# Own buffers for one batch's local queries and keys, a packed third Fourier tile, and a later place for one output scaling

## The chip, the cores and the metric

The kernel runs on one core of a Trainium2 chip. The metric is the device time of one execution in microseconds (us), as the median of several runs; less is better. One execution was also recorded by the hardware profiler, and the rows further down are from that one.

A core has engines that each work through an instruction stream of their own in order: TensorE (PE in the profile; PEld is its weight load, which overlaps), VectorE (DVE), ScalarE (ACT), GpSimd (POOL), and SyncE (SP), which here only issues transfers. Streams wait for each other by semaphores. Transfers are carried by 16 DMA engines.

## What is computed

```python
# q, k, v: 4 batches x 8 heads x 576 x 64
rel = pos[:, None] - pos[None, :]
mask_local = (rel >= 0) & (rel < 32)                       # heads 0 to 3
mask_strided = (rel >= 0) & (pos[None, :] % 32 == pos[:, None] % 32)   # heads 4 to 7
x = softmax(where(mask, q @ k.T / 8, -1e9)) @ v            # 576 x 512 for each batch
u = x + real(fft(fft(x, axis=1), axis=2))                  # over sequence and channels
un = (u - mean(u)) / sqrt(var(u) + 1e-6)
x2 = u + relu(un @ w_ch1) @ w_ch2                          # 512 -> 2048 -> 512
h = relu(x2.T @ w_tok1) @ w_tok2                           # over the sequence, 576 -> 256 -> 576
u2 = x2 + h.T
out = u2 + relu(u2 @ w_ch3) @ w_ch4                        # 512 -> 1536 -> 512
```

All is float32. The big weights come as pairs of 32-bit words, from which the kernel builds its numbers on ACT, DVE and POOL.

## The kernel before

**Attention, the first 147 us.** Each batch has six groups (`Group`, 24 in the list `gl`): three of local heads, each with two tiles of 96 queries against a window of 128 keys, and three of strided heads, where the positions are ordered so that those with equal remainder by 32 stand together (tiles of 126 or 108 positions). A group computes scores on PE (`scores`: a matmul that puts the mask into PSUM, then one per head and tile, `sc<-k,qz`), the maximum on DVE and the exponentials on ACT (`softmax`), transposes the result on PE (`trans`, tile `tp`), multiplies it by the values (`av`), and scales by the sum of the exponentials (`out`, on DVE, lines L262 to L264). `out` also stores the rows to the scratch `xd`. Two heads share 128 partitions of `k`. So that one matmul takes one head alone, the query tile `qz` has zeros in the other head's 64 rows; the zeros are set once at the start (L518), and the loads write the live rows only.

**The loads of queries and keys.** `load_qk(b, g, pool)` issues for batch b two loads of `qz[g]` and one of the keys `k`; g is 0 for local and 1 for strided heads. Both kinds have one buffer, so a load waits until the scores of the batch before have read it. In the loop over the groups the local set of the next batch is loaded in front of a batch's fourth group, and its strided set in front of its own first group. All these loads are on SP, in program order with the stores of `xd`, the loads and stores of the Fourier stage and the weight loads `wraw` (L101). The program gives SP's transfers eight completion counters in turn, so an issue also waits for the transfer that stands eight places before it. The constants `cs`, `ss`, `cd`, `sd` (cosines and sines as high and low parts) are issued by POOL's queue behind the values of the first batch.

**The Fourier stage (`Fourier`).** While batch b+1 is in attention, batch b is transformed; the fourth batch's transform stands in the MLP stage behind. `load` reads `xa` (rows from the front of the sequence) and `xr` (the mirror rows) in three tiles of 128, 128 and 33 rows; `prep` adds them to `e` on DVE and splits the sum in a high part (ACT, L317) and a low part (POOL, L318) in the tile `f`; `s1` multiplies by the cosines or sines in five column blocks (`g<-cs,f`, L334): in each of the first four there are nine matmuls, three tiles by high x high, high x low, low x high, and the fifth block, one column, has six. `s2` multiplies over the channels and stores the three tiles of `u` to the scratch `ud`. When these steps come is set by a small table in `fft(b)`, which ties each of them to a group's matmul or reduction.

**The first norm and the MLP.** In group 17's turn the first three tiles of `u` are loaded (`us`, L447), in group 19's turn `ln_stats` computes their mean and inverse root on DVE (L471 and, in `inverse_root`, a chain of small instructions that ends at L478); groups 20 to 22 apply it, and behind the last group the tiles are transposed to `uT`, which opens the MLP: `h<-uT,wAh` (L413), `hh` on ACT (L417), `hl` on DVE (L418), `oo` (L432). Here PE multiplies high and low parts, three products each. The second block (token mixing and its own MLP) follows.

The order in which the instructions of one engine stand is worked out by a scheduler when the kernel is built, from the program's order, the dependences and the ties given by `behind`.

## Time and profile before

| | us |
|---|---|
| three runs | 926.74, 932.41, 928.37 |
| median | 928.37 |
| profiled execution, its own time | 922.47 |
| its span, first to last instruction | 920.7 |
| PE busy | 892.5 (97%) |
| DVE busy | 560.0 (61%) |
| ACT busy | 408.3 (44%) |
| POOL busy | 313.0 (34%) |

161 MB were moved. The mean granted clock of PE was 0.994 of full speed, which is the upper of its two levels (2.4 GHz). Busy shares are means over stages with different limits; PE's 97% leaves 28 us of the span without PE work, start and end included.

### The profile page before, as it was taken

Reading aid. Unit: us, or ns where it says so; the run is one execution under the profiler, and the core shown is the slowest. Engines: PE = TensorE matmul, PEld = TensorE weight load, DVE = VectorE, ACT = ScalarE, POOL = GpSimd, SP = SyncE. Lnnn points to the kernel's source line nnn. Section 1 sums busy time; section 2 is a strip of 40 time slices with the busy share of each in tenths; the row PEclk is TensorE's granted clock in tenths of the full one; section 3 lists DMA queues with packets and bytes.
Section 4 is the critical chain, followed back from the end, with each engine's and each line's share of the span. In section 5 each row is a group of like instructions: output and inputs, shape, how many; then the busy total and the mean of one; then the engine's idle time right before and its main releaser. Section 6 shows DMA issues by size and latency. Waiting matters only on the chain.

```text
span 920.7 us, 15422 instructions
## 1 busy us (share of the span) xinstructions
PE 892.5 (97%) x5554; PEld 824.2 (90%) x5554; DVE 560.0 (61%) x1046; ACT 408.3 (44%) x1069; POOL 313.0 (34%) x372
## 2 busy tenths in 40 slices
PE   7989989999999999999999999999999999999997
PEld 6979988999998989998888897777899999999997
DVE  4667979798894434443443446645434444888774
ACT  5978776353442333233223224323455545444432
POOL 3122222332330133344444333422223001946660
PEclk9989999999999999999999999999999999999999
DMA  9997864234431354644744665579833287156351
GB/s 260 282 289 216 255 205 136 98 127 146 138 111 68 99 160 146 196 128 126 220 141 136 209 200 180 176 262 313 293 120 147 104 270 243 36 161 222 125 203 47
DMA packets 116972, 161.00 MB, mean 175 GB/s; under 512 B 9662, under 2 KB 70180, under 8 KB 116896
## 3 DMA queue, kind: packets, MB, share of 16 engines
q1 hardware_dynamic: 114928, 157.29, 54.0%
q0 software_dynamic: 1712, 2.51, 1.1%
q8 instruction: 44, 0.72, 0.3%
q14 instruction: 32, 0.26, 0.1%
q10 hardware_dynamic: 256, 0.21, 0.1%
HBM read 104.92 MB, written 55.06 MB: 174 GB/s over the span
## 4 chain that ended last, share of the span: by engine, by line
PE 63%; DVE 11%; DMA 9%; ACT 5%; issue 4%; POOL 4%; SPq 3%; POOLq 0%; DVEq 0%; ACTq 0%
PE oo L1036 14%; PE oo L432 10%; PE h L413 10%; PE z L895 8%; PE y L895 4%; DMA wraw<-in_w1b_dram 4%; POOL wt L147 3%; PE tu L806 3%; PE tk L784 3%; PE sc L211 2%; PE w L895 2%; SPq L101 2%; DVE wu L112 2%; DVE wu L108 2%; DVE wu L113 2%
## 5 line engine op out<-in xcount | busy, mean ns | idle before, releaser
L413 PE MATMUL h<-uT,wAh 128*128 128x384 f32 x768 | 203.1, 337 | 0.2
L413 PEld LDWEIGHTS h<-uT,wAh 128*128 128x128 f32 x768 | 139.0, 188 | 5.2 <-PE g L334 0.4
L1036 PE MATMUL oo<-wo,ht 128*128 128x256 f32 x972 | 133.7, 281 | 0.0
L413 PE MATMUL h<-uT,wAl 128*128 128x384 f32 x384 | 129.0, 336 | 0.0
L1036 PEld LDWEIGHTS oo<-wo,ht 128*128 128x128 f32 x972 | 126.5, 189 | 0.0
L432 PE MATMUL oo<-wAh,hh 128*128 128x512 f32 x288 | 113.9, 398 | 4.3 <-ACT hh L417 4.2
L432 PE MATMUL oo<-wAl,hh 128*128 128x512 f32 x288 | 113.7, 395 | 0.0
L432 PE MATMUL oo<-wAh,hl 128*128 128x512 f32 x288 | 104.4, 396 | 0.2 <-DVE hl L418 0.2
L418 DVE SCALAR_TENSOR_TENSOR hl<-h,hh 128x384 fp32r<-128x384 f32 x96 | 52.6, 552 | 76.0 <-ACT hh L417 75.8
L108 DVE TENSOR_SCALAR wu<-wu 128x512 f32<-128x512 f32 (+1 forms) x62 | 38.5, 622 | 78.2 <-ACT wu L106 73.2
L124 POOL TENSOR_TENSOR wAl<-wu,wAh 128x512 fp32r<-128x512 f32 x32 | 45.9, 1437 | 104.3 <-ACT wAh L123 104.3
L417 ACT ACTIVATE hh<-h 128x384 fp32r<-128x384 f32 x96 | 45.9, 484 | 70.4 <-PE h L413 68.9
L147 POOL TENSOR_TENSOR wt<-wu 128x128 f32<-128x128 f32 x48 | 21.1, 461 | 158.3 <-DVE wu L113 158.3
L413 PEld LDWEIGHTS h<-uT,wAl 128*128 128x128 f32 x384 | 72.1, 188 | 2.8
L432 PEld LDWEIGHTS oo<-wAh,hh 128*128 128x128 f32 x288 | 54.1, 188 | 15.6 <-ACT hh L417 6.6
L106 ACT ACTIVATE wu<-wraw 128x512 f32<-128x512 f32 (+1 forms) x62 | 41.0, 662 | 60.6 <-DMA wraw<-in_w1b_dram 46.9
L895 PE MATMUL z<-ut,wo 128*128 128x384 f32 x324 | 64.5, 338 | 1.7 <-DVE ut L863 1.7
L432 PEld LDWEIGHTS oo<-wAh,hl 128*128 128x128 f32 x288 | 53.8, 188 | 13.7 <-DVE hl L418 1.3
L432 PEld LDWEIGHTS oo<-wAl,hh 128*128 128x128 f32 x288 | 54.1, 188 | 8.9
L230 ACT ACTIVATE sm<-sc,st 96x128 f32<-96x128 f32 (+2 forms) x176 | 61.6, 373 | 0.6
L895 PEld LDWEIGHTS z<-ut,wo 128*128 128x128 f32 x324 | 56.4, 188 | 2.1 <-DVE ut L863 2.0
L211 PE MATMUL sc<-k,qz 128*96 128x128 f32 (+2 forms) x352 | 51.0, 283 | 5.3 <-DMA k<-in_kt_dram 5.3
(197 smaller groups left out, 1840.9 us busy)
## 6 DMA issues: line engine op xcount, KB each, us to landing
wo<-wsd SPq DMA_DIRECT2D x84, 256.0 KB
wsd<-wraw SPq DMA_DIRECT2D x24, 448.0 KB
wsd<-wbl SPq DMA_DIRECT2D x24, 448.0 KB
u<-u2d SPq DMA_DIRECT2D x36, 256.0 KB
hd<-hs SPq DMA_DIRECT2D x12, 768.0 KB
hw<-hd SPq DMA_DIRECT2D x36, 256.0 KB
wraw<-in_w1a_dram SPq DMA_DIRECT2D x16, 512.0 KB
wraw<-in_w2a_dram SPq DMA_DIRECT2D x16, 512.0 KB
```

Source lines behind the costliest of these rows:

```text
L106: behind(nc.scalar.activation(out=f32(u), in_=f32(high), func=AF.Abs, scale=2.0**16), relu.get("hh"))
L108: clamp = eng().tensor_scalar(f32(u), f32(u), E_MIN, E_MAX, op0=ALU.max, op1=ALU.min)
L124: nc.gpsimd.tensor_tensor(out=lo[:, :n], in0=u, in1=f32(hi[:, :n]), op=ALU.subtract)
L147: nc.gpsimd.tensor_tensor(out=o, in0=x, in1=y, op=ALU.add if plus else ALU.subtract)
L211: last = nc.tensor.matmul(out=sc[:q, j * k:(j + 1) * k], lhsT=qz[self.g][:, e, hp, qs], rhs=k_t[self.b, self.g][:, hp, ks], start=False, s ...
L230: self.exp = nc.scalar.activation(out=smv[:, j, :], in_=sc[:, j, :], func=AF.Exp, scale=SCALE, bias=st[:, 1, j:j + 1], accum_out=st[:, 2, ...
L413: nc.tensor.matmul(out=h[:, :384], lhsT=l[:, ws], rhs=r[:, kd, :], start=x == 0, stop=x == 11)
L417: relu["hh"] = nc.scalar.activation(out=hh, in_=h[:, :384], func=AF.Relu)
L418: relu["hl"] = nc.vector.scalar_tensor_tensor(out=hl, in0=h[:, :384], scalar=0.0, in1=f32(hh), op0=ALU.max, op1=ALU.subtract)
L432: nc.tensor.matmul(out=self.o[c][i], lhsT=l[:, s], rhs=r, start=first and x == 0, stop=last and x == 2)
L895: Unit.last = nc.tensor.matmul(out=bank[:, :384], lhsT=w[:, c + kd * P:c + kd * P + P], rhs=r[:, kd], start=first and x == 0, stop=x == 5, ...
L1036: nc.tensor.matmul(out=acc[G][bank][:, 256 * half:256 * half + 256], lhsT=lh[:, i], rhs=w[:, c:c + 256], start=m == 0 and x == 0 and half ...
```

## The change

1. *Buffers.* The local keys `k` have two buffers instead of one, and the second batch's local queries go to four tiles of their own, `qo`, which lie in buffers that `u` uses later. Their zeros are set at the start like those of `qz`. The second batch's local set is loaded at the start of the program (`load_qk(1, 0, ap)`); in the loop, the first batch's fourth group now loads the third batch's local set, and the third batch's fourth group the fourth's. The second batch's fourth group loads none.
2. *Third Fourier tile.* The rows are regrouped: tiles 0 and 1 hold rows 1 to 256 (and their mirror rows), tile 2 the 33 rows left. The high and low parts of tile 2 share one operand `f3` of 128 partitions (rows 0 to 32 the high part, 64 to 96 the low part, and from 96 on, over the low part's last row, the high part again), with a fifth constant tile that holds the matching rows; one matmul then does what three did (in the one-column block two). ACT writes one more copy for each batch. Because the 33 rows are no longer one piece in memory, `load` and the stores of tile 2 have six transfers each; tiles 0 and 1 have one for each half. `cs` and `ss` are one transfer each instead of four.
3. *Scaling.* The 21st group's scaling (`out` of `gl[20]`) is put behind the last instruction of the first norm's chain.

```diff
-        t = pool.tile([P, 2, S], F32, tag=f"k{g}", name="k", bufs=(1, 1)[g])
+        t = pool.tile([P, 2, S], F32, tag=f"k{g}", name="k", bufs=(2, 1)[g])
         k_t[b, g] = t
+        own = b == 1 and g == 0
         for ps in ([slice(0, 1), slice(1, 2)] if b == 0 and g < 1 else [slice(0, 2)]):
             for e in range(2):
                 r = slice(64 * e, 64 * e + 64)
-                nc.sync.dma_start(out=qz[g][r, e, ps], in_=a["qt"][b, g, r, ps])
+                if own:
+                    for hp in range(2):
+                        nc.sync.dma_start(out=qo[e, hp][r], in_=a["qt"][b, g, r, hp])
+                else:
+                    nc.sync.dma_start(out=qz[g][r, e, ps], in_=a["qt"][b, g, r, ps])
...
-                nc.vector.tensor_scalar_add(rs, rs, 1e-9)
+                behind(nc.vector.tensor_scalar_add(rs, rs, 1e-9), self.prev)
...
+        def rows(self, i):
+            xa, xr = self.x[i]
+            if i < 2:
+                return (xa, 0, 1 + 128 * i, 128), (xr, 0, 288 + 128 * i, 128)
+            return ((xa, 32, 0, 1), (xa, 1, 257, 15), (xa, 16, 272, 16),
+                    (xr, 0, 575, 1), (xr, 1, 544, 15), (xr, 16, 559, 16))
...
-            behind(nc.scalar.activation(out=f[:n, 0, i], in_=e[:n], func=AF.Copy), prev2)
-            nc.gpsimd.tensor_tensor(out=f[:n, 1, i], in0=e[:n], in1=f32(f[:n, 0, i]), op=ALU.subtract)
+            h, l = (f[:, 0, i], f[:, 1, i]) if i < 2 else (f3[0:33], f3[64:97])
+            behind(nc.scalar.activation(out=h, in_=e[:n], func=AF.Copy), prev2)
+            if i == 2:
+                behind(nc.scalar.activation(out=f3[96:128], in_=e[0:32], func=AF.Copy), prev2)
+            nc.gpsimd.tensor_tensor(out=l, in0=e[:n], in1=f32(h), op=ALU.subtract)
...
-            for i in range(3):
+            for i in range(2):
+                h, l = f[:, 0, i, c], f[:, 1, i, c]
                 if mt < 4:
-                    h, l = f[:, 0, i, c], f[:, 1, i, c]
-                    mats += [(h, w[0][:, i], m), (h, w[1][:, i], m), (l, w[0][:, i], m)]
+                    mats += [(h, w[:, i], m), (h, w[:, 2 + i], m), (l, w[:, i], m)]
                 else:
-                    mats += [(f[:, :, i, 256], w[0][:, i], 2), (f[:, 0, i, 256:257], w[1][:, i], 1)]
+                    mats += [(f[:, :, i, 256], w[:, i], 2), (h, w[:, 2 + i], 1)]
+            mats.append((f3[:, c], w[:, 4], 128 if mt < 4 else 1))
...
-            na = min(n, 288 - r0)
-            nc.sync.dma_start(out=ud[self.b][287 + r0:287 + r0 + n, :], in_=xr[:n])
-            nc.sync.dma_start(out=ud[self.b][r0:r0 + na, :], in_=xa[:na])
+            for t, p0, r0, k in self.rows(i)[::-1]:
+                nc.sync.dma_start(out=ud[self.b][r0:r0 + k, :], in_=t[p0:p0 + k])
...
+        for e in range(2):
+            for hp in range(2):
+                qo[e, hp] = lp.tile([P, S], F32, tag="u", name="qo", bufs=6)
+                nc.vector.memset(qo[e, hp][64 - 64 * e:128 - 64 * e], 0.0)
         load_vl(0)
         load_qk(0, 1, ap)
         vlast = load_vs(0)
-
-        cs = [fp.tile([P, 3, 290], F32R, name=f"cs{i}") for i in range(2)]
-        ss = [fp.tile([P, 3, 290], F32R, name=f"ss{i}") for i in range(2)]
+        load_qk(1, 0, ap)
+
+        cs, ss = (fp.tile([P, 5, 290], F32R, name=nm) for nm in ("cs", "ss"))
...
+        for t, nm in ((cs, "cs"), (ss, "ss")):
+            nc.gpsimd.dma_start(out=t, in_=a[nm])
         for i in range(2):
-            for t, w in ((cs[i], a["cs"][i]), (ss[i], a["ss"][i])):
-                nc.gpsimd.dma_start(out=t[:, 0:2], in_=w[:, 0:2])
-                nc.gpsimd.dma_start(out=t[:33, 2], in_=w[:33, 2])
...
             if gi == 3 and b + 1 < B:
-                load_qk(b + 1, 0, ap)
+                if b != 1:
+                    load_qk(2 if b == 0 else 3, 0, ap)
                 load_vl(b + 1)
...
             if gno == 19:
                 mvs = ln_stats(us, lp, g.red[1])
+                gl[20].prev = relu["ln"]
```

The rows of the order below are an engine's instructions as they stand one behind the other: the line in the kernel, the operation, output and inputs with the shape, and a count where like rows follow each other. The line numbers of the changed kernel are its own.

The first place is SP's stream in the opening, behind the first batch's loads and up to the keys of the second batch's strided set. Here `qz_140` is the local query tile and `qz_139` the strided one, and `xd` are the first batch's stores. Before:

```order
L101 DMA wraw<-in_w1a_dram 128x1024
L101 DMA wraw<-in_w2a_dram 128x1024
L101 DMA wraw<-in_w1a_dram 128x1024
L176 DMA qz_140<-in_qt_dram 64x1152
L271 DMA xd_69<-x 96x2x256
L176 DMA qz_140<-in_qt_dram 64x1152
L177 DMA k<-in_kt_dram 128x1152
L271 DMA xd_69<-x 96x2x256
L180 DMA vl<-in_vl_dram 128x1536
L271 DMA xd_69<-x 96x2x256
L176 DMA qz_139<-in_qt_dram 64x1152 x2
L177 DMA k<-in_kt_dram 128x1152
```

And now:

```order
L179 DMA qo<-in_qt_dram 64x576 x4
L182 DMA k<-in_kt_dram 128x1152
L101 DMA wraw<-in_w1a_dram 128x1024
L101 DMA wraw<-in_w2a_dram 128x1024
L101 DMA wraw<-in_w1a_dram 128x1024
L181 DMA qz_140<-in_qt_dram 64x1152
L277 DMA xd_69<-x 96x2x256
L181 DMA qz_140<-in_qt_dram 64x1152
L182 DMA k<-in_kt_dram 128x1152
L277 DMA xd_69<-x 96x2x256
L185 DMA vl<-in_vl_dram 128x1536
L277 DMA xd_69<-x 96x2x256
```

The four `qo` loads and a set of keys, which are the second batch's, stand ahead of all; the pair of `qz_140` and the keys that follow it stand where they stood, and now carry the third batch's rows. The strided set follows these rows, as before.

The second place is SP at the end of the first batch's Fourier transform: its last stores of `u` (`ud`) and the loads of the first norm (`u`). Before:

```order
L376 DMA ud_73<-xa 32x512
L101 DMA wraw<-in_w1a_dram 128x1024
L375 DMA ud_73<-xr 33x512
L447 DMA u<-ud_73 128x512
L183 DMA vs<-in_vs_dram 126x1280
L447 DMA u<-ud_73 128x512
L277 DMA xd_71<-x 9x6x256
L278 DMA xd_71<-x 9x6x256
L447 DMA u<-ud_73 64x512
```

And now:

```order
L388 DMA ud_73<-xa 16x512
L388 DMA ud_73<-xa 15x512
L388 DMA ud_73<-xr 16x512
L388 DMA ud_73<-xr 15x512
L388 DMA ud_73<-xr 1x512
L388 DMA ud_73<-xa 1x512
L283 DMA xd_71<-x 9x6x256
L284 DMA xd_71<-x 9x6x256
L459 DMA u<-ud_73 128x512 x3
```

Six stores stand where two stood, and the three loads of `u` stand behind the two `xd` stores, where two of them stood ahead.

The third place is DVE at the end of the attention, from the last instructions of the norm's chain (`nr`, `mv`); `x<-av,st` is a group's scaling, `xa<-xa,m` belongs to the Fourier stage. Before:

```order
L464 SCALAR_TENSOR_TENSOR mv<-nr,mv 128x3
L478 SCALAR_TENSOR_TENSOR mv<-mv 128x3
L264 TENSOR_TENSOR x<-av,st 96x512
L367 TENSOR_TENSOR m<-sa,fb 128x258
L368 TENSOR_TENSOR m<-sa,fb 128x258
L373 TENSOR_TENSOR xa<-xa,m 128x512
L373 TENSOR_TENSOR xr<-xr,m 128x512
L227 TENSOR_REDUCE st<-sc 126x4
L312 TENSOR_TENSOR w<-xa,xr 128x510
L313 TENSOR_TENSOR e<-xa,xr 128x2
L315 TENSOR_TENSOR e<-w 128x255
L264 TENSOR_TENSOR x<-av,st 96x512
```

And now:

```order
L474 SCALAR_TENSOR_TENSOR nr<-mv,nr 128x3
L269 RECIPROCAL st<-st 108x4
L475 TENSOR_TENSOR nr<-nr,mv 128x3
L476 SCALAR_TENSOR_TENSOR mv<-nr,mv 128x3
L490 SCALAR_TENSOR_TENSOR mv<-mv 128x3
L268 TENSOR_SCALAR st<-st 96x8
L269 RECIPROCAL st<-st 96x8
L270 TENSOR_TENSOR x<-av,st 96x512
L270 TENSOR_TENSOR x<-av,st 126x512
L270 TENSOR_TENSOR x<-av,st 108x512
L270 TENSOR_TENSOR x<-av,st 108x256
L415 TENSOR_TENSOR uT<-ut,uT 128x4x128 x3
```

Before, the scalings of the last groups were spread between other work; now four of them stand in a row behind the norm's chain and ahead of the instructions that form `uT`.

## Rows read from the trace of the kernel before

**Rows 1.** The page's 40 slices of the span, busy tenths of PE in each.
```profile
PE   7989989999999999999999999999999999999997
```

**Rows 2.** The waits of PE, of SP in 8:60, of DVE in 40:170: us, times, longest.
```profile
PE sc L211 <- DMA k<-in_kt_dram: 5.3, 2, 4.4
...
PE oo L432 <- ACT hh L417: 4.2, 6, 1.1
...
SPq L278 <- DMA k<-in_kt_dram: 1.0, 1, 1.0
...
DVE bs L471 <- DMA u<-ud: 3.4, 2, 2.6
```

**Rows 3.** The timeline of PE: start us, duration us, instruction, idle time before it.
```profile
7.73 4.65 PE L211 MATMUL sc<-k,qz 128*96 128x128 f32 x24 [0.93 <-DMA k<-in_kt_dram]
...
39.03 1.04 PE L211 MATMUL sc<-k,qz 128*96 128x128 f32 x8
...
43.25 1.04 PE L211 MATMUL sc<-k,qz 128*126 128x126 f32 x8
...
55.02 0.46 PE L205 MATMUL sc<-mask_l,ident_r 96*96 96x512 f32 x1
...
59.83 1.99 PE L211 MATMUL sc<-k,qz 128*96 128x128 f32 x8 [4.36 <-DMA k<-in_kt_dram]
...
147.52 1.39 PE L413 MATMUL h<-uT,wAh 128*128 128x384 f32 x3
```

**Rows 4.** Windows: engines' busy us (instructions), then granted clock, DMA share, GB/s.
```profile
8.00:40.00 32.00, 31.82 (x283) 29.96 (x283) 17.41 (x40) 27.43 (x143) 7.23 (x14) 1.00 1.11 305
...
44.00:48.00 4.00, 4.00 (x43) 3.93 (x42) 2.59 (x6) 4.00 (x19) 1.27 (x1) 1.00 0.46 119
...
60.00:64.00 4.00, 4.00 (x19) 3.85 (x20) 1.50 (x6) 0.82 (x3) 0.00 (x0) 0.50 1.04 411
...
64.00:68.00 4.00, 4.00 (x33) 3.93 (x32) 3.48 (x8) 2.30 (x14) 1.29 (x1) 0.78 1.04 253
...
70.00:110.00 40.00, 38.84 (x349) 37.11 (x348) 35.23 (x74) 31.39 (x139) 10.27 (x8) 1.00 0.79 239
```

**Rows 5.** The timeline of POOL's and SP's transfer issues: start us, duration of the issue.
```profile
31.79 0.54 POOL L541 DMA_DIRECT2D sd<-in_sd_dram  x1
...
42.81 0.75 SPq L278 DMA_DIRECT2D xd<-x  x1
...
52.98 0.57 SPq L177 DMA_DIRECT2D k<-in_kt_dram  x1
...
110.98 0.33 SPq L375 DMA_DIRECT2D ud<-xr  x1
```

**Rows 6.** Transfers issued in 0:60: count, KB each, us from issue to landing.
```profile
qz<-in_qt_dram SPq DMA_DIRECT2D x10, 288.0 KB
...
k<-in_kt_dram SPq DMA_DIRECT2D x5, 576.0 KB
...
cs<-in_cs_dram POOLq DMA_DIRECT2D x2, 290.0 KB, 11.1
...
cs<-in_cs_dram POOLq DMA_DIRECT2D x2, 37.4 KB, 11.1
...
sd<-in_sd_dram POOLq DMA_DIRECT2D x2, 258.0 KB, 12.2
```

**Rows 7.** Lines by form in 0:221: busy us, mean ns, idle before.
```profile
L317 ACT ACTIVATE f<-e 33x512 fp32r<-33x512 f32 x4 | 2.5, 628 | 1.1 <-DVE e L316 1.1
...
L518 DVE MEMSET qz<- 64x576 f32 x4 | 2.2, 538 | 0.7 <-issue 0.7
```

**Rows 8.** The chain that ended last: start us, duration us, piece.
```profile
109.96 1.76 DMA ud<-xa
...
144.45 0.52 ACT f L317
...
192.63 2.42 PE g L334 x18
```

More of the change, by code (lines that the diff above doesn't have):

```diff
@@ L211, in scores @@
                         last = nc.tensor.matmul(
-                            out=sc[:q, j * k:(j + 1) * k], lhsT=qz[self.g][:, e, hp, qs],
+                            out=sc[:q, j * k:(j + 1) * k], lhsT=(qo[e, hp] if (self.b, self.g) == (1, 0) else qz[self.g][:, e, hp])[:, qs],
                             rhs=k_t[self.b, self.g][:, hp, ks], start=False, stop=j == n - 1)
@@ L291, in load @@
             self.x[i] = xa, xr
-            na = min(n, 288 - r0)
             if i == 2:
-                nc.gpsimd.memset(xa[32:33], 0.0)
-            if i == 0:
-                nc.gpsimd.memset(xr[0:1], 0.0)
-            nc.sync.dma_start(out=xa[:na], in_=xd[self.b][r0:r0 + na, :])
-            for c0, c1 in ([(1, 16), (16, n)] if i == 0 else [(0, n)]):
-                self.last = nc.sync.dma_start(out=xr[c0:c1], in_=xd[self.b][287 + r0 + c0:287 + r0 + c1, :])
+                nc.gpsimd.memset(xa[0:1], 0.0)
+                nc.gpsimd.memset(xr[32:33], 0.0)
+            for t, p0, r0, n in self.rows(i):
+                self.last = nc.sync.dma_start(out=t[p0:p0 + n], in_=xd[self.b][r0:r0 + n, :])
+        def rows(self, i):
[4 more added lines that the diff above has]
+                    (xr, 0, 575, 1), (xr, 1, 544, 15), (xr, 16, 559, 16))
         def prep(self, i, prev=None, prev2=None):
-            r0, n = ST[i]
-            f = self.f = self.k["f"]
+            n = NR[i]
+            f, f3 = self.k["f"]
             xa, xr = self.x[i]
@@ L441, in u_tile @@
             if c % 3 < 2:
-                return self.lp.tile([P, DM], F32, tag="u", name="u", bufs=6)
+                return self.lp.tile([P, S], F32, tag="u", name="u", bufs=6)[:, :DM]
             return self.pool.tile([P, DM], F32, tag="v", name="v", bufs=3)
@@ L477, in ln_stats @@
             nc.vector.reciprocal(out=mv[:, :n, 3], in_=mv[:, :n, 2])
-        nc.vector.scalar_tensor_tensor(out=mv[:, :n, 2], in0=mv[:, :n, 0], scalar=-1.0, in1=mv[:, :n, 3],
-                                       op0=ALU.mult, op1=ALU.mult)
+        relu["ln"] = nc.vector.scalar_tensor_tensor(out=mv[:, :n, 2], in0=mv[:, :n, 0], scalar=-1.0,
+                                                    in1=mv[:, :n, 3], op0=ALU.mult, op1=ALU.mult)
         return [mv[:, i] for i in range(n)]
@@ L527, in attention_fourier_mlp_kernel @@
         alt = fp.tile([P, 258], F32R, name="alt")
-        f = fp.tile([P, 2, 3, 512], F32R, name="f")
+        f = fp.tile([P, 2, 2, DM], F32R, name="f"), fp.tile([P, DM], F32R, name="f3")
         g4 = [fp.tile([P, 290], F32R, name=f"g4{x}") for x in "hl"]
@@ L531, in attention_fourier_mlp_kernel @@
         tc.add_manual_dep(tick.ins, vlast.ins.name, mybir.DependencyInfo(mybir.DependencyClass.Sync, mybir.DependencyReason.DATA), reason="constants behind the first batch")
-        for t in (g4[1], alt, f[:, 0, 2], f[:, 1, 2], cs[0][:, 2], cs[1][:, 2], ss[0][:, 2], ss[1][:, 2]):
+        for t in (g4[1], alt, f[1][32:64]):
             nc.gpsimd.memset(f32(t), 0.0)
@@ L601, in attention_fourier_mlp_kernel @@
             if gno == 17:
-                us = [u_rows(T, lp.tile([P, DM], F32, tag="u", name="u", bufs=6)) for T in range(3)]
+                us = [u_rows(T, lp.tile([P, S], F32, tag="u", name="u", bufs=6)[:, :DM]) for T in range(3)]
             if gno == 21:
-                us += [u_rows(T, lp.tile([P, DM], F32, tag="u", name="u", bufs=6)) for T in range(3, 6)]
+                us += [u_rows(T, lp.tile([P, S], F32, tag="u", name="u", bufs=6)[:, :DM]) for T in range(3, 6)]
             if gno == 19:
                 mvs = ln_stats(us, lp, g.red[1])
+                gl[20].prev = relu["ln"]
             if 20 <= gno < 23:
@@ L828, in u_load @@
         def u_load(T):
-            u = lp.tile([P, DM], F32, tag="u", name="u", bufs=6)
+            u = lp.tile([P, S], F32, tag="u", name="u", bufs=6)[:, :DM]
             nc.sync.dma_start(out=u, in_=u2d[T // 9][T % 9])
@@ L1054, in halves @@
                 if G == Gs[-1]:
-                    k = lp.tile([P, DM], F32, tag="u", name="k", bufs=6)
+                    k = lp.tile([P, S], F32, tag="u", name="k", bufs=6)[:, :DM]
                     nc.scalar.activation(out=k, in_=t, func=AF.Copy)
@@ L1157, in trig @@
         return v
-    s = np.arange(289)
+    s = np.concatenate([np.arange(1, 257), [288], np.arange(257, 288), [0]])
+    for nm, f in (("cs", np.cos), ("ss", np.sin)):
+        w = np.zeros((289, 290))
+        w[:, :289] = trig(f, 576, s, s)
+        h, l = _split(w)
+        t = np.zeros((P, 5, 290), np.float32)
+        t[:, 0:2], t[:, 2:4] = (x[:256].reshape(2, P, 290).transpose(1, 0, 2) for x in (h, l))
+        t[0:33, 4], t[64:97, 4], t[97:128, 4] = h[256:], h[256:], l[257:288]
+        c[nm] = t
     full = {}
-    for nm, f in (("cs", np.cos), ("ss", np.sin)):
-        w = np.zeros((384, 290))
-        w[:289, :289] = trig(f, 576, s, s)
-        full[nm] = w.reshape(3, P, 290).transpose(1, 0, 2)
     d, k = np.arange(256), np.arange(257)
```

15 lines of the change are left out of this document (7 added, 8 removed).

## The prediction

> **What bounds the kernel now.** The page's slices come first [rows 1]: of TensorE's (PE's) 40 digits every one from the seventh to the last but one is a 9. So time can be taken from two things only: PE work that stands in PE-bound stretches, and the few places where PE waits. Among PE's waits [rows 2] the longest single one behind the start-up is one of 4.4 us for `k`, in the attention stage, the first 147 us (the first `h` matmul starts at 147.52 [rows 3]). The timeline shows the wait: at 55.02 PE starts the mask of the third batch's first local scores, ends it at 55.48, and waits 4.36 us for that batch's keys. Then it runs slowly: eight score matmuls take 1.99 us where the same eight take 1.04 at 39.03. The windows [rows 4] give the reason: the granted clock is 0.50 in 60 to 64 us and 0.78 in 64 to 68, which is the lower level (1.2 GHz) after idle PE. Half of 4 us and 0.22 of 4 us are 2.9 us lost, so this stall costs 4.4 + 2.9 = 7.3 us.
>
> Why are the keys late? Before the change `qz` and `k` of the local heads have one buffer each, so the load waits for the second batch's local scores and stands on SP (the DMA-issuing queue) behind the Fourier loads: it is issued at 52.98 [rows 5]. But the second reason matters more here: the DMA engines are full in 8 to 40 us (share 1.11 [rows 4]). The strided keys of the second batch, needed at 43.25 [rows 3], are just in time. SP's issues share eight completion counters in turn, so an issue waits for the one eight places before; the `xd` store at 42.81 is eight places behind these keys, and SP's waits up to 60 us have one wait of that line for `k`, of 1.0 us [rows 2, 5]. So the keys landed at about 42.75, half a microsecond before use.
>
> **The change part by part.** *(1) Own buffers.* The wait at 55.5 goes: the third batch's q and k are now issued where the second's were, at 16 to 20 us, 30 us before use. That takes 7.3 us away. What is late next is the second batch's strided keys, as the order of SP shows: its own local set (2 x 288 + 576 = 1152 KB [rows 6]) is now issued at the start, and the third batch's, as large, still stands ahead of the strided set. So 1152 KB more must pass before those keys. The constants grow too: from 2 x (290 + 37.4) KB for `cs` [rows 6] and the same for `ss`, 1310 KB, to 2 x 128 x 1450 x 4 bytes = 1450 KB. Together 1292 KB or 1.32 MB, at the 305 GB/s that the full DMA engines moved in 8 to 40 us [rows 4], are 4.3 us. The keys then land at 42.75 + 4.3 = 47.1, and PE wants them at 43.25: a new stall of 3.8 us. I price the slow clock behind it like that behind the old one, 2.9 us, since both are idle stretches of about 4 us. The new stall is 6.7 us, and of the 7.3 us only 0.6 is kept. Bounds: without a new stall -7.3. With the keys later still +0.6: the last large constant landed at 31.79 + 12.2 = 44.0 us [rows 5, 6], so 1.2 us of other transfers may come ahead of the keys, 5.0 + 2.9 - 7.3. I take -0.6, since the landing at 42.75 and the full DMA are both measured. ScalarE can't fill the hole: it is busy in 4.00 of 4 us at 44 to 48 [rows 4].
>
> The page "DMA: Bandwidth & Descriptors" of the Trainium skill (section "Queues, rings and completion order") says that each DMA engine takes turns between the queues that have work for it. By that the constants, which POOL's queue now issues without a wait between two parts, take turns with the strided set earlier than before, and the change would come out at the upper bound just given; the trace of before can't show it, since there the constants were issued in two parts.
>
> The four added memsets of `qo` follow the eight of `qz` at the start of VectorE (DVE), 0.54 us each [rows 7], 6.5 us in all; DVE's first reduction waits for scores that start at 7.73 us [rows 3], so they cost nothing.
>
> *(2) Packed third tile.* Each batch's first stage drops from 9 matmuls to 7 in four column blocks and from 6 to 5 in the fifth: 9 fewer, 36 in all. Eighteen in a row take 2.42 us [rows 8], so one is 0.134 us. The fourth batch's nine stand in the MLP stage, where PE has no gaps: -1.2. Of the third batch's, five stand behind the first `h` matmuls: -0.7. The other 22 (2.9 us) stand in the attention stage, where DVE is about as full as PE (35.2 and 38.8 of 40 us in 70 to 110 [rows 4]); I count half, -1.5, with bounds -2.9 and 0. Added: four ScalarE copies of 0.63 us [rows 7]. Three have gaps to go into; the third batch's stands in the chain that opens the MLP stage (the copy at 144.45 [rows 8]): +0.5, bounds 0 and +1.6 (that one and two more). On SP each batch issues 10 loads for 7 and 10 stores for 6. Where it counts is the first batch: the first norm's loads of `u` now stand behind all six stores of tile 2. Four more at about 0.4 us [rows 5] are +1.6 on a path for which DVE already waited 3.4 us [rows 2]; the norm's statistics also stand some instructions later on DVE, so I take +0.8, bounds 0 and +1.6.
>
> *(3) The 21st group's scaling.* It now stands behind the whole chain of the norm, and with it the 22nd's and 23rd's: three multiplications of 0.6 us in a row ahead of the last one and of `uT`. DVE has the same instructions there as before; what is lost is overlap with the last transposes, which wait for these PSUM buffers. +0.5, bounds 0 and +3.
>
> Sum: -0.6 - 1.2 - 0.7 - 1.5 + 0.5 + 0.8 + 0.5 = -2.2 us. Behind the attention stage PE has no gap that a shift could sink into: its largest wait there is 4.2 us in six pieces, for `hh` [rows 2]. The profiled execution took 922.47 us (span 920.7); it becomes 920.3. The median of the runs shown is 5.9 us above the profiled one; I take the same 2.2 off: **926.2 us**. With all the small terms at their lower ends it would be 923.0, with all terms at their upper ends 933.3; those don't fall together, and this case's own range is 923 to 931.
>
> **The rivals.** *A: the stall vanishes.* The second batch's strided keys still come in time, because the rings are not served in the order of issue, or less is queued at that moment than I add up. Then -7.3 - 1.2 - 0.7 - 1.5 + 1.8 = -8.9: 919.5 us (916 with the small terms at their lower ends, 922 with some of them at their upper ones). For it: the DMA has gaps at 44 to 48 us (0.46 [rows 4]), so a small delay is cheap. Against: the margin was half a microsecond, and 1.32 MB can't pass for nothing.
>
> *B: slower, by the small transfers.* If the small stores of tile 2 don't overlap but wait for each other, each costs its landing of 1.76 us [rows 8] and not its issue of 0.4: four more are 7.0 us on the loads of `u`, and DVE, which stands in order at the statistics, holds every PE group behind it. It decides from the point where this wait exceeds the 3 us by which the statistics stand later. Of the sum the +0.8 goes and +7.0 and a slow clock of 2.9 come: -2.2 - 0.8 + 9.9 = +6.9, 935.3 us. Against: SP issued the two stores of tile 2 at 109.96 and 110.98, with a third transfer between them, sooner than one landing [rows 5, 8]. The same page of the skill ("Anatomy of one DMA") puts a constant part of about 2.0 us on each transfer; taken as a price per transfer this rival would be 1 us dearer, but nothing in it says that they don't overlap.
>
> *C: the packing is hidden.* If DVE alone sets the attention stage, the 22 matmuls there are worth nothing: -0.7, 927.7 us, inside the forecast's own ends.
>
> **How the numbers follow.** Forecast 0.45, A 0.27, B 0.15, C 0.13. The range reaches into both sides until about 0.05 of A and 0.1 of B are left out: **917 to 934**. A measurement of this kernel can tell about 1% (9.3 us) from no change. Faster by more than that is below 919.1, half of A: 0.14. Slower by more is above 937.7, B's far end: 0.04. The same: 0.82.
>
> **What the profile after would show.** Step by step: no wait for `k` near 55 us; instead one of 3 to 4.5 us at about 43 us, at the second batch's first strided scores, and a granted clock of about 0.5 behind it; first-stage blocks of 14 and not 18; DVE's wait for `u` at 3 to 6 us; the first `h` matmuls at 145 to 147 us (147.5 before [rows 3]). The prediction is wrong if there is no such wait at 43 us (then A), or if the first `h` matmul comes later than 149 us (then B or something at the end of attention that I have not seen).

## The result and the profile after

The changed kernel took 938.63 us (median of 12 runs, 931.69 to 942.14); the kernel before, in 12 runs in all, 925.12. The ratio is 1.0129, 95% interval 1.0100 to 1.0157: slower by 1.3%, where 0.2% faster was forecast, and outside the stated range. A second set of runs (e10 below) gave 1.0134. The profiled execution has a span of 929.8 us against 920.7; it was the fastest of its 12, so it shows less than the typical loss: 9.1 us, where the medians lie 13.5 us apart.

The whole span can be cut at the first and the last `h` matmul. The windows of the kernel before (columns as in [rows 4]), up to the first `h`, the MLP up to the last `h`, and the rest:

```profile
7.50:147.50 140.00, 129.47 (x1123) 122.68 (x1124) 102.54 (x243) 109.75 (x495) 34.68 (x35) 0.96 0.83 245
147.50:576.70 429.20, 424.78 (x2209) 382.44 (x2208) 247.61 (x468) 150.72 (x293) 146.54 (x188) 1.00 0.48 147
576.70:920.70 344.00, 336.66 (x2223) 318.37 (x2222) 205.51 (x327) 145.62 (x278) 125.68 (x132) 1.00 0.53 181
```

The same of the changed kernel:

```profile
7.50:152.00 144.50, 130.13 (x1102) 124.33 (x1100) 106.51 (x246) 112.27 (x500) 32.14 (x29) 0.93 0.77 235
152.00:585.50 433.50, 424.50 (x2193) 380.29 (x2194) 250.08 (x468) 150.79 (x294) 146.21 (x188) 1.00 0.48 145
585.50:929.80 344.30, 336.74 (x2223) 318.34 (x2221) 206.53 (x327) 145.52 (x278) 126.99 (x132) 1.00 0.53 182
```

Up to the first `h` PE has 21 matmuls fewer and yet is busy 0.7 us longer, because the mean granted clock fell from 0.96 to 0.93; and it is idle 14.4 us (144.50 less 130.13) instead of 10.5. In the MLP, 16 matmuls fewer, it is idle 9.0 us instead of 4.4. The rest is equal to 0.3 us. So +4.5, +4.3 and +0.3 us make the +9.1 of the two profiles.

The page's slices of PE, answering to [rows 1], now have 8 where 9 stood in the second (23 to 46 us), the fifth and the seventh (93 to 116 and 139 to 163 us), and in the 25th, far in the MLP:

```profile
PE   7899888999999999999999998999999999999997
```

Where PE waits now, the view of waits (us in total, times, longest), first up to 60 us, then 100 to 152, then 152 to 300; these lines answer to [rows 2]:

```profile
PE av L259 <- DMA vl<-in_vl_dram: 2.6, 1, 2.6
PE sc L217 <- DMA k<-in_kt_dram: 0.2, 1, 0.2
...
PE g L347 <- DVE gl L357: 5.1, 1, 5.1
PE av L259 <- ACT pt L246: 2.9, 1, 2.9
PE h L425 <- DVE uT L415: 1.2, 1, 1.2
...
PE h L425 <- ACT wAh L123: 1.3, 1, 1.3
PE oo L444 <- ACT wAh L123: 0.8, 1, 0.8
```

The wait of 4.4 us for `k` is gone. In its place stand 2.6 us for the second batch's local values. The costliest, 5.1 us for `gl`, stood in the kernel before as well, but shorter; there it was

```profile
PE g L334 <- DVE gl L344: 1.8, 1, 1.8
```

The timeline of PE now shows the waits for `vl`, `gl` and `pt`, and the first `h`, which was at 147.52 [rows 3]:

```profile
43.29 1.51 PE L259 MATMUL av<-vl,pt 128*96 128x64 f32 x8 [2.64 <-DMA vl<-in_vl_dram]
...
118.45 1.37 PE L347 MATMUL g<-cs,f 128*2 128x290 f32 x5 [5.08 <-DVE gl L357]
...
142.01 3.14 PE L259 MATMUL av<-vs,pt 108*108 108x64 f32 x16 [2.88 <-ACT pt L246]
...
151.97 0.41 PE L425 MATMUL h<-uT,wAh 128*128 128x384 f32 x1 [1.21 <-DVE uT L415]
```

Each idle stretch has a stretch at a lower granted clock behind it or in it, as the windows show (columns as in [rows 4]):

```profile
40.00:48.00 8.00, 5.36 (x34) 5.09 (x33) 2.45 (x6) 4.18 (x24) 0.00 (x0) 0.68 0.83 210
112.00:120.00 8.00, 2.92 (x20) 2.22 (x19) 3.58 (x9) 2.27 (x11) 2.25 (x3) 0.87 0.71 237
120.00:128.00 8.00, 8.00 (x57) 7.89 (x57) 6.04 (x16) 5.27 (x26) 0.00 (x0) 0.70 0.61 179
136.00:144.00 8.00, 5.06 (x37) 4.57 (x36) 8.00 (x20) 5.25 (x19) 2.95 (x3) 0.86 0.38 127
144.00:152.00 8.00, 6.27 (x40) 5.82 (x39) 6.09 (x15) 4.88 (x10) 2.63 (x3) 0.71 0.26 73
```

In the kernel before, the first of these windows had the full clock; the wait for `gl` had a shorter slow stretch behind it there too:

```profile
40.00:48.00 8.00, 8.00 (x83) 7.82 (x82) 4.93 (x11) 7.72 (x38) 1.27 (x1) 1.00 0.60 179
120.00:128.00 8.00, 7.53 (x56) 6.85 (x57) 5.38 (x22) 5.78 (x24) 0.00 (x0) 0.79 0.76 245
```

The `gl` for which PE waits 5.1 us was not late by itself: DVE, which makes it, stood in order at the norm's first statistics, waiting 5.8 us for `u` (2.6 at most before [rows 2]). DVE's and SP's timelines at that place (SP's rows are issues):

```profile
116.42 0.69 DVE L483 BATCH_NORM_STATS2 bs<-u 128x6 f32<-128x512 f32 x1 [5.77 <-DMA u<-ud]
...
105.67 0.42 SPq L188 DMA_DIRECT2D vs<-in_vs_dram  x1
106.22 0.36 SPq L101 DMA_DIRECT2D wraw<-in_w1a_dram  x1
106.67 1.16 SPq L388 DMA_DIRECT2D ud<-xa  x2
107.92 1.10 SPq L388 DMA_DIRECT2D ud<-xr  x3
109.06 0.24 SPq L388 DMA_DIRECT2D ud<-xa  x1
111.49 0.77 SPq L283 DMA_DIRECT2D xd<-x  x1
112.72 0.75 SPq L284 DMA_DIRECT2D xd<-x  x1
113.57 1.35 SPq L459 DMA_DIRECT2D u<-ud  x3
```

The first stage's blocks are of 14 matmuls, and the six small stores are issued in 2.6 us, both as forecast. But `vs` (630 KB) and `wraw` (512 KB) now stand ahead of all six stores; before, `vs` stood behind the two stores and behind a load of `u` (the second place in "The change"). And with six stores, the two `xd` stores stand eight places behind `vs` and `wraw`, and must wait for these to land. SP's waits say so:

```profile
SPq L283 <- DMA vs<-in_vs_dram: 2.1, 1, 2.1
SPq L284 <- DMA wraw<-in_w1a_dram: 0.4, 1, 0.4
```

All three loads of `u` queue behind: the first is issued at 113.57, 7.9 us behind `vs`. Two of them stood ahead of the `xd` stores before.

### The profile page after: what moved, and what is told of

It is laid out like the page before. It is cut to its first block, busy times and chain, and to the rows that moved or that the text cites. A ratio compares the mean times of both kernels' runs of the same rounds, so it can differ in the third digit from the quotient of the medians.

```text
span 929.8 us, 15382 instructions
## 1 busy us (share of the span) xinstructions
PE 893.4 (96%) x5518; PEld 824.1 (89%) x5518; DVE 568.2 (61%) x1050; ACT 410.8 (44%) x1073; POOL 310.1 (33%) x361
## 4 chain that ended last, share of the span: by engine, by line
PE 49%; DVE 19%; DMA 12%; issue 5%; ACT 5%; POOL 4%; SPq 4%; DVEq 0%; POOLq 0%; ACTq 0%
PE oo L1053 14%; PE z L912 8%; PE oo L444 6%; PE h L425 5%; PE y L912 4%; DMA wraw<-in_w1b_dram 3%; POOL wt L147 3%; DVE wu L112 3%; PE tu L823 3%; PE tk L801 3%; DVE wu L108 3%; DVE wu L113 3%; SPq L101 2%; PE w L912 2%; DMA vl<-in_vl_dram 2%
## 5 line engine op out<-in xcount | busy, mean ns | idle before, releaser
L124 POOL TENSOR_TENSOR wAl<-wu,wAh 128x512 fp32r<-128x512 f32 x32 | 43.0, 1346 | 125.8 <-ACT wAh L123 117.3
L113 DVE SCALAR_TENSOR_TENSOR wu<-wraw,wu 128x512 int32<-128x512 int32 (+1 forms) x62 | 48.9, 791 | 1.0
```

Source lines behind the costliest of these rows:

```text
L113: v.scalar_tensor_tensor(out=u, in0=low, scalar=29, in1=u, op0=ALU.logical_shift_right, op1=ALU.bitwise_or)
L124: nc.gpsimd.tensor_tensor(out=lo[:, :n], in0=u, in1=f32(hi[:, :n]), op=ALU.subtract)
```

## The experiments

Each ran beside the kernel before; "ratio" is to that kernel, with its 95% interval. "First h" and "MLP" (first to last `h`) come from one profile each; two profiles of the changed kernel differ by 4.9 us at the first `h` (e10), so the comparisons go by the ratios, and profiles only show what PE waits for. The profiles of the changed kernel, e8 and e15 are the fastest of their runs, that of e9 is the second slowest. The ratios come from several sets of runs, each with its own runs of the kernel before; the difference of two ratios has an interval of some 0.35% to either side (0.5% with e2, e4 or e10), 3 to 5 us.

| kernel | ratio (interval) | first h, us | PE idle to it | MLP, us |
|---|---|---|---|---|
| before | 1 | 147.5 | 10.5 | 429.2 |
| changed | 1.0129 (1.0100 to 1.0157) | 152.0 | 14.4 | 433.5 |
| e1 packing alone | 1.0071 (1.0045 to 1.0096) | 152.4 | 16.8 | 430.4 |
| e2 packing, tie | 1.0118 (1.0073 to 1.0164) | 154.3 | 15.1 | 432.8 |
| e3 buffers, packing | 1.0069 (1.0041 to 1.0096) | 153.6 | 15.1 | 428.7 |
| e4 e3 + chain held together | 1.0101 (1.0061 to 1.0142) | 153.4 | 16.8 | 433.1 |
| e5 e3 without row 0, 127 rows | 1.0173 (1.0148 to 1.0198) | 160.2 | 24.6 | 434.2 |
| e6 e3 + tile order 2, 0, 1 | 1.0038 (1.0019 to 1.0057) | 148.3 | 15.0 | 432.3 |
| e7 e3 + keys later | 1.0062 (1.0040 to 1.0084) | 149.6 | 15.2 | 430.8 |
| e8 e6 + e7 | 1.0015 (0.9993 to 1.0037) | 140.4 | 9.7 | 432.9 |
| e9 e3 without row 0 | 1.0074 (1.0046 to 1.0103) | 155.0 | 15.6 | 436.9 |
| e10 changed, again | 1.0134 (1.0097 to 1.0171) | 156.9 | 19.7 | 434.8 |
| e11 e7 + order 0, 2, 1 | 1.0019 (0.9997 to 1.0042) | 147.6 | 12.6 | 431.6 |
| e12 e8 + u earlier | 1.0018 (0.9996 to 1.0041) | 143.6 | 9.4 | 435.6 |
| e13 e1 + idle matmuls | 1.0032 (1.0013 to 1.0051) | 148.8 | 13.5 | 431.6 |
| e14 e1, three transfers | 1.0013 (0.9992 to 1.0033) | 146.7 | 11.6 | 433.0 |
| e15 e11 + tie | 0.9997 (0.9979 to 1.0016) | 141.9 | 8.3 | 432.2 |
| e16 e11 + u earlier | 0.9970 (0.9947 to 0.9994) | 144.0 | 10.7 | 429.8 |
| e17 e16 + tie | 1.0007 (0.9988 to 1.0027) | 145.1 | 10.3 | 433.4 |
| e18 e16, again | 0.9990 (0.9967 to 1.0012) | 143.6 | 10.4 | 430.1 |

**The parts, e1 to e3.** Own buffers alone don't fit into the on-chip memory without what the packing frees. So the parts are taken out of the changed kernel. Without the tie:

```diff
-                gl[20].prev = relu["ln"]
```

Without the buffers: `bufs=(1, 1)[g]`, no `qo`, no `load_qk(1, 0, ap)` at the start, and `load_qk(b + 1, 0, ap)` in the loop.

e1, expected: 

> Packed third tile alone; the local keys and queries as before the change, no tie of the scaling. Theory P (the packing is what costs: with six small stores the loads of u for the first norm stand behind two stores of xd, the norm's chain on DVE is drawn out to the end of attention, and the MLP opens late): slower than before by 5 to 12 us, the first h matmul at 150 to 154 us. Theory O (the packing is a gain, and the tie of the scaling and the loads of the opening cost): 2 to 4 us faster than before, the first h matmul at 145 to 147 us.

e2, expected: 

> Packed tile and the tied scaling, without the own buffers. Theory P: as e1 within 2 us, since the tie only delays scalings that the drawn-out chain delays anyway. Theory O with the tie as the cause: slower than e1 by 4 us or more. The wait for the third batch's keys at 55 us is there again in both.

e3, expected: 

> Own buffers and packed tile, the scaling not tied. Theory P: within 2 us of the changed kernel, so still 8 to 14 us slower than before; the buffers keep 0 to 3 us against e1. If the tie is the cause: 4 us or more faster than the changed kernel.

Packing alone costs 0.71%, 6.5 us. The buffers add nothing to it that can be told from noise (e3 against e1, -0.0002). The tie adds 0.0047 without the buffers and 0.0060 with them, 4.3 to 5.5 us; that is against theory P, which gave it 2 at most. No run has the tie in the kernel before. By the order that the scheduler makes, it would be nearly nothing there: it moves rows in one stretch of 14 on DVE and none on any other engine. With the packing it moves rows on every engine.

**The chain held together, e4.** On the changed kernel:

```diff
-                gl[20].prev = relu["ln"]
+                gl[21].prevr = relu["ln"]
...
+            behind(self.red[-1], self.prevr if e == 1 else None)
```

Expected: 

> As the changed kernel, but instead of the scaling of the 21st group the second maximum of the 22nd group stands behind the norm's chain, which keeps the chain's instructions on DVE together (it ends some 40 instructions earlier in DVE's stream). Theory P: the chain ends at 125 to 130 us instead of 146.7, the first h matmul comes at 146 to 148.5 us instead of 152, and the run is 4 to 7 us faster than the changed kernel. If the late chain is not the cause, within 2 us of the changed kernel.

The chain ended at 133.9 us instead of 146.6 (123.8 before the change), and the first `h` still came at 153.4. The run is 0.28% below the changed kernel and 0.32% above e3, both within the noise. So my first theory, that the drawn-out chain makes the MLP open late, fell. In e4, as in the changed kernel, e2 and e10, PE waits 1.3 and 0.8 us in the MLP for `wAh`, the high part of a weight tile that ACT makes (L123); in e1, e3 and e7, which hold no tie, it doesn't, and their MLP takes 428.7 to 430.8 us against 432.8 to 434.8. But this wait is not the whole of it, nor the tie's alone: e12, e14 and e17 further down have none, and their MLP takes 433.0 to 435.6; e9, without a tie, has one of 1.4 us.

**Row 0 and the order of the tiles, e5, e6 and e9.** The regrouping puts row 0 into the last tile, so the first tile of `u` depends on the last stores. e5 and e9 take that row from row 1 (on e3):

```diff
+            for c0, c1, x in ((0, 1, 1), (1, 16, 0), (16, n, 0)) if T == 0 else ((0, n, 0),):
+                nc.sync.dma_start(out=u[p0 + c0:p0 + c1], in_=ud[b][r0 + c0 + x:r0 + c1 + x, :])
```

(e5 with pieces of 1 and 127 rows.) e6 is e3 with

```diff
-                yield p[0], lambda i=i, p=p: four_b.s2(i, group(*p, "mm"))
+                yield p[0], lambda i=(i + 2) % 3, p=p: four_b.s2(i, group(*p, "mm"))
```

e5, expected: 

> Base e3 (own buffers, packed tile, no tie). The first row of the norm's first tile of u is loaded from row 1 instead of row 0, so one row of the first batch's result is wrong; the first two tiles of u then don't depend on the six stores of the packed tile, and their loads stand ahead of those again, as before the change. Theory U (regrouping put row 0 into the last tile, so all statistics of the first norm wait for the last stores; PE stands 5.5 us behind them at 114 to 120 us, runs slowly after it, and the chain ends at the end of attention): DVE's longest wait for u falls from 6.2 to under 3 us, the chain ends before 135 us, the first h matmul comes at 146 to 150 us instead of 153.6, and the run is 4 to 8 us faster than e3. If the wait for u only fills time that the attention's end would lose anyway: within 2 us of e3.

e6, expected: 

> Base e3, with the second Fourier stage of each of the first three batches in the order of tiles 2, 0, 1, so that the six small stores go first and all rows are right. Theory U: as e5, 4 to 8 us faster than e3, the wait for u under 3 us. If six small stores cost by their number wherever they stand: no faster than e3.

e9, expected: 

> As e5 (base e3, the first row of the first tile of u taken from row 1, so one row is wrong), but the tile is loaded in pieces of 1, 15 and 112 rows. In e5 the piece of 127 rows took some 12 us to land and held the stores behind it, so e5 told nothing of row 0. Theory U: DVE's longest wait for u under 3.5 us, the chain ends before 138 us, and the run is 3 to 7 us faster than e3. Rival (it is the loads' place behind the last stores of any tile): within 2 us of e3.

e5 told of something else: DVE waited 12.6 us for the piece of 127 rows, which was issued at 109.05. The timelines of DVE and SP:

```profile
121.88 0.69 DVE L486 BATCH_NORM_STATS2 bs<-u 128x6 f32<-128x512 f32 x1 [12.63 <-DMA u<-ud]
...
109.05 3.66 SPq L462 DMA_DIRECT2D u<-ud  x2
112.81 0.72 SPq L188 DMA_DIRECT2D vs<-in_vs_dram  x1
113.58 0.57 SPq L388 DMA_DIRECT2D ud<-xa  x1
114.25 1.12 SPq L388 DMA_DIRECT2D ud<-xr  x3
115.41 6.68 SPq L388 DMA_DIRECT2D ud<-xa  x2
```

The last of these issues stands eight places behind that load and waits 6.1 us for it, until 121.9. In e9, with 15 and 112 rows, DVE's longest wait for `u` fell to 2.6 us, as before the change, and the chain ended at 137.4; but the time is that of e3. In its profile DVE still waits 5.0 us in all for `u` (3.4 before, 6.2 in e3) and PE 4.0 us for `gl` (5.5 in e3). So row 0 taken out of the last tile gives nothing back, and theory U in that form fell; e9's two more loads and its other order are not separated from it. e6 is 0.31% (3 us) faster than e3, less than theory U wanted and at the edge of the noise, and not by the theory's step: DVE's longest wait for `u` is 4.7 us and not under 3, and 7.6 in all where e3 has 6.2.

**The opening, e7 and e8.** e7 is e3 with

```diff
+                prev = load_qk(b, 1, ap)
+                if b == 1:
+                    load_qk(2, 0, ap, prev)
```

where the three transfers stand `behind` the second batch's strided keys. e8 has e6's edit as well.

e7, expected: 

> Base e3, with the third batch's local queries and keys issued behind the second batch's strided set instead of ahead of it. Theory Q (the 1.3 MB more in the opening delay what stands behind them: the values of the second batch's local heads come 2.8 us late and PE runs slowly after it): the wait for the values at 43 us is gone, PE's mean clock in 40 to 60 us is over 0.95 instead of 0.83, and the run is 3 to 6 us faster than e3. Rival (the transfers ahead of the values, the weights and the second batch's own local set, are what delays them): the wait shrinks by less than half, within 2 us of e3.

e8, expected: 

> e6 and e7 together. If both theories hold and add: 7 to 13 us faster than e3, so 1 to 7 us faster than before the change.

The wait for the values went, and the clock is 1.00 in 40 to 60 us, as theory Q had it; but the run is only 0.07% faster, not 3 to 6 us. In the profiles the first `h` comes 4.0 us earlier than in e3 and the MLP takes 2.1 us more. A part of the gain went into the next wait, for the first batch's Fourier operand. PE's timeline and windows of e7:

```profile
59.92 0.53 PE L349 MATMUL g<-cs,f 128*128 128x290 f32 x2 [2.47 <-ACT f L329]
...
56.00:60.00 4.00, 1.53 (x14) 1.25 (x12) 2.49 (x7) 0.97 (x3) 0.06 (x1) 1.00 0.99 303
60.00:64.00 4.00, 3.49 (x26) 3.14 (x27) 3.97 (x12) 4.00 (x16) 3.27 (x3) 0.82 0.91 313
```

L329 is the copy of the operand's high part, L317 before, and not the copy that the packing adds (L331). It was late because DVE, which adds up `e`, had waited 5.2 us for the rows `xr`. Together (e8) the two edits are worth 0.54% of e3, 5 us, where 7 to 13 were expected.

**The changed kernel again, e10.** Expected: 

> The changed kernel once more, on the chip and beside the runs of before of this call, with a second profile; its first profile was its fastest of 12 runs (931.7 against a median of 938.6). Expected: ratio 1.010 to 1.016, and in a profile near the median the same waits with a lower granted clock behind them (below 0.9 in more of the stretches of 20 us in the first 160 us).

As expected in the ratio and the waits: 5.8 us (`gl`) and 2.9 us (`pt`) again, and the first `h` at 156.9. Against the expectation the clock is below 0.9 in no more stretches than in the first profile: in the same three of 20 us, 40 to 60 and 120 to 160.

**The order of tiles 0, 2, 1, and u earlier, e11, e12 and e16.** e11 is e7 with `(0, 2, 1)[i]` for the tile in `s2`. e12 and e16 are e8 and e11 with

```diff
+            if gno == 16:
+                us = [u_rows(T, lp.tile([P, S], F32, tag="u", name="u", bufs=6)[:, :DM]) for T in range(1)]
             if gno == 17:
-                us = [u_rows(T, lp.tile([P, S], F32, tag="u", name="u", bufs=6)[:, :DM]) for T in range(3)]
+                us += [u_rows(T, lp.tile([P, S], F32, tag="u", name="u", bufs=6)[:, :DM]) for T in range(1, 3)]
```

e11, expected: 

> Base e7 (own buffers, packed tile, no tie, third batch's local set later), with the second Fourier stage of the first three batches in the order of tiles 0, 2, 1. The weight conversions of the MLP then stand where they stood before the change (the ninth behind the 5th hh on ACT, in e8 behind the 7th). Theory M (the changed orders also shift those conversions, PE waits for wAh, and the MLP takes 432 to 434 us instead of 429 to 431): first h to last h in 427 to 430 us, and with the first h at 139 to 145 us the run is 4 to 9 us faster than before the change. Rival (the MLP takes back whatever the attention gains, since DVE bounds its opening): first h to last h 432 us or more, within 3 us of before.

e12, expected: 

> As e8 (s2 in the order 2, 0, 1 and the third batch's local set later), with the load of the norm's first tile of u written one group earlier in the program; the ninth conversion stands behind the 6th hh. Theory U: wait for u under 3.5 us (4.9 in e8). Theory M: first h to last h in 428 to 431 us. Together 2 to 6 us faster than e8. Rival: within 2 us of e8.

e16, expected: 

> Base e11, with the first tile of u loaded one group earlier in the program; the MLP's conversions stand as before the change. A version to beat the kernel before: 1 to 5 us faster than e11, so 0 to 4 us faster than before the change. Rival (the attention is bound by DVE behind the waits): as e11.

Conversions are the steps that build the MLP's weights from pairs of words. e11 is 0.43% faster than e7, but no faster than before; it has no wait for `wAh`, and its MLP still takes 431.6 us, so theory M explains at most a part. e12 is as e8: DVE's longest wait for `u` fell from 4.9 to 2.2 us, but in the profiles the first `h` came later (143.6 against 140.4, the latter from e8's fastest run) and the MLP took 435.6. e16 is 0.49% faster than e11 and below the kernel before.

**What in the packing costs, e13 and e14.** e13 (on e1) does the first two matmuls of a block twice (a further line, not shown, starts the sum anew behind the extra ones):

```diff
+            nd = 2 if mt < 4 else 1
+            mats = mats[:nd] + mats
```

e14 (on e1) has three loads and three stores for tile 2, and one small memset on POOL fewer:

```diff
-            return ((xa, 32, 0, 1), (xa, 1, 257, 15), (xa, 16, 272, 16),
-                    (xr, 0, 575, 1), (xr, 1, 544, 15), (xr, 16, 559, 16))
+            return (xa, 32, 0, 1), (xa, 0, 256, 32), (xr, 0, 544, 32)
```

e13, expected: 

> Base e1 (packing alone), with the first two matmuls of each block of the first stage done twice (one in the last block), so that PE has as many matmuls as before the change; the transfers are the packed tile's, the results are right. The scheduler then ends the norm's chain on DVE at row 219 instead of some 250. Theory W (the matmuls saved are worth their time and the transfers cost): slower than e1 by 2 to 5 us. Theory V (what costs is the order that comes with the packing, above all the drawn-out chain and the idle stretches of PE with the lower clock behind them; the saved matmuls only make room for waits): within 2 us of e1 or faster.

e14, expected: 

> Base e1, with the third tile in three loads and three stores (of 1, 32 and 32 rows) instead of six; the pieces of 32 rows begin one row earlier than they should, so the transform is wrong, and the work is the same. SP's order at the loads of u is that of e1 but for the three stores. If the number of small transfers costs: 3 to 6 us faster than e1, the wait for u at least 1.5 us shorter than 6.1. If it does not: within 2 us of e1.

e14 is 0.58% faster than e1, 5.3 us of the 6.5, with some 3 us of noise to either side. SP's order at the loads of `u` is that of e1 less three stores; its timeline, and DVE's and SP's waits:

```profile
104.56 0.42 SPq L188 DMA_DIRECT2D vs<-in_vs_dram  x1
105.10 0.36 SPq L101 DMA_DIRECT2D wraw<-in_w1a_dram  x1
105.55 0.72 SPq L386 DMA_DIRECT2D ud<-xa  x2
106.37 0.31 SPq L386 DMA_DIRECT2D ud<-xr  x1
106.77 0.76 SPq L283 DMA_DIRECT2D xd<-x  x1
107.59 0.75 SPq L284 DMA_DIRECT2D xd<-x  x1
111.05 1.30 SPq L457 DMA_DIRECT2D u<-ud  x3
...
DVE bs L481 <- DMA u<-ud: 3.6, 2, 3.3
SPq L457 <- DMA ud<-xa: 2.6, 1, 2.6
```

The `xd` stores no longer wait for `vs` and `wraw`; the loads of `u` wait 2.6 us for the `ud` stores, which they must. DVE's wait for `u` is 3.6 us, in e1 6.1. But the place eight behind is not all of it. The first load of `u` is issued 6.5 us behind `vs` here (104.56 to 111.05), 7.9 us in the changed kernel and 8.1 in e1 (106.48 to 114.59), so that place and the issues themselves are worth 1.4 to 1.6 us. In all three `vs` and `wraw` stand ahead of the stores: here the store that the load waits for landed some 5 us after its issue at 105.55 or 105.97, where one of tile 2 took 1.76 before [rows 8]. And e14's streams stand in another order too: in PE's rows, as the two traces have them one behind the other, some 800 of 5518 matmuls stand elsewhere than in e1. Which part of the 5.3 us is whose isn't separated.

And e13, with 36 matmuls more than e1, is 0.39% faster (3.6 us, just clear of noise). It keeps the six stores behind `vs` and `wraw`, and the first `xd` store still waits 1.1 us for `vs`, as in e1; yet DVE's wait for `u` is

```profile
DVE bs L485 <- DMA u<-ud: 2.9, 1, 2.9
```

and PE's for `gl` 1.4 us, in e1 5.4. In e13 a scaling (`x<-av,st`) and two steps of a weight (`wu`) stand on DVE ahead of the first statistics; in e1 these stand behind them and wait with them. So the order that comes with the packing costs more than the 36 matmuls saved are worth; that these are worth nothing isn't shown, since e13 changes both.

**The tie alone, e15 and e17, and the best version, e18.** e15 and e17 are e11 and e16 with the tie; e17 is thus the changed kernel with three moves of transfers and stores.

e15, expected: 

> Base e11, with the 21st group's scaling tied behind the norm's chain as in the change. The chain ends some 30 rows earlier on DVE than in the changed kernel, so the tie holds the scaling for less. If the tie costs by itself: 3 to 6 us slower than e11. If it costs only together with the drawn-out chain: within 2 us of e11.

e17, expected: 

> The changed kernel with all three parts, the tie too, and with three moves: second Fourier stage in the order of tiles 0, 2, 1, the first tile of u loaded one group earlier in the program, the third batch's local set behind the second's strided set. If the tie costs nothing where the chain is not drawn out (as e15 said): within 2 us of e16. If it costs by itself: 3 us or more slower than e16.

e18, expected: 

> e16 once more on another set of runs, to see whether it beats the kernel before: ratio 0.994 to 0.999. If e16 was luck of its chip: 0.999 to 1.003.

The tie is worth -0.22% on e11 (e15) and, in the same set of runs, +0.17% on e18 (e17): neither can be told from zero. Against e16's own set e17 is 0.37% slower, 3.4 us, where 2 were expected at most; e16 and e18 are the same kernel, so a small cost is not excluded. It cost 4.3 to 5.5 us in the packing's first order. e18 confirms that e16 is no slower than before; that it is faster (0.9970, then 0.9990 with an interval that reaches 1.0012) is likely and not certain.

## Why the prediction was wrong

**What held.** Part 1: the wait at 55 us went, and one at 43 us came in its place, with a slow clock behind it; it goes again when the third batch's set is issued later (e7), so the backlog makes it. The victim was not the strided keys but the local values, issued between the third batch's set and these keys: 2.6 us of idle time and a clock of 0.68 in 8 us. Forecast was a net of -0.6 us; measured -0.2 (e3 against e1) and +1.0 (changed against e2), each with an interval of 3 to 5 us. That the two stalls about cancel agrees with these; that they cost 7.3 and 6.7 us is not shown, since taking the new one away (e7) gave 0.6 us. Rival A (no new stall) fell.

**The step that failed is part 2**: its terms add up to -2.1 us, and the packing alone took +6.5 (e1). Two terms are wrong. *The stores, +0.8, bounds 0 and +1.6.* I priced four more issues at 0.4 us each. Their issues do cost that. What I left out is what stands ahead of them: `vs` and `wraw`, for which the loads of `u` wait twice. The stores land behind these two, and by the rule that I had stated myself in my second paragraph (an issue waits for the transfer eight places before it) six stores instead of two put the stores of `xd`, with the loads of `u` behind them, eight places behind them. Half as many transfers give back 5.3 us (e14), but the eight places and the issues make only 1.4 to 1.6 us of the lateness of the loads; the rest is not separated from the other order that e14's streams have. Rival B named DVE's wait at `u`, the PE groups held behind it and the slow clock, and had the sign; its mechanism, landings that don't overlap, was not it (the first load of `u` needs row 0, the last of the six stores in SP's order, and is issued 6.9 us after the first of them; six landings of 1.76 one behind the other would be 10.6), and my argument against it (two stores issued sooner than one landing) spoke only against that mechanism.

*The matmuls, -1.2, -0.7 and -1.5.* With the 36 put back the kernel is 3.6 us faster (e13). I took a PE without gaps as a PE whose work can be subtracted. The edits here make the scheduler put the streams in another order, and the MLP took 428.7 to 436.9 us in these kernels with the same 16 matmuls fewer, against 429.2 before (one profile each). *The added copy, +0.5*, shows no cost: ACT makes the third batch's at 143.00 to 143.63 and then waits 3.2 us for the norm's chain.

**Part 3, +0.5, bounds 0 and +3, was mis-sized**: in the order that the packing made, the tie measured +4.3 and +5.5. With other orders (e15, e17: -2.0 and +1.6 us) it is not told from zero, and the +0.5 not refuted. In the packing's order the tied kernels wait for `wAh` in the MLP, which takes 2.4 us longer in e2 than in e1 and 4.8 in the changed kernel than in e3; and at the end of attention PE waits 2.9 us for `pt`, 1.6 in e1 and 0.9 in e3. The rest of the tie's cost there I can't place.

The prediction's own sign for being wrong, a first `h` later than 149 us, was met. Above 937.7, where the median lies, it had put a chance of 0.04.

**What stays open.** Why e9 gains nothing though DVE's longest wait for `u` is as before the change; why the MLP's length moves by up to 8 us between these profiles (late conversions are a part, and two profiles of the changed kernel differ by 1.3); and how much of the gain of e6, e11 and e14 is the place of the transfers and how much the new order: each of these edits changes both, and no run holds the order and changes the transfers alone. What is shown is that the work is not the cause: the changed kernel and e17 have the same work, and 1.2% lies between them. The sum of terms was not the right model.

## What to carry to other kernels

Where a queue's issues share a few completion counters, more small transfers can cost more than their own issues: look which large transfers stand ahead of them, and what now stands as many places behind a large one as there are counters. Work taken from a full engine need not show in the time when a scheduler rebuilds the order: put the work back idle and see which way the time moves, and look whether the order moved with it. And after a change that lost, move the transfers before dropping it: the same work with three moves was 11 us faster than the change as it stood, level with the kernel before.

## What was not expected of the hardware

DVE waited 12.6 us for a load of 127 rows of 2 KB (254 KB), and 2.6 us at most for pieces of 15 and 112 rows of the same tile (e5, e9). The new stalls of 2.6 to 5.1 us each had a stretch of 8 us at a mean clock of 0.68 to 0.71 in or behind them. By an estimate from the first of these windows, the stall of 2.6 us cost nearly double its length (0.32 of 8 us more); the run without it (e7) got only 0.6 us of that back.
